# A second-stage projection as seven products of quarters in place of eight, and a new order at the seam of two stages

## The chip, the cores and the metric

The kernel runs on one core of one Trainium2 chip. The metric is the device time of one execution in microseconds (us). The kernel before takes 581.78 us, the median of three runs (581.43 to 581.80).

## What is computed

Three layers follow each other on 1536 tokens of 512 features, in float32. The first is a linear attention with decay. The second and third are what the change touches:

```
g = xn @ w_gate ; x = (g * sigmoid(g) * (xn @ w_val)) @ w_out           # 512 -> 1536 -> 512
h = max(x @ w1, x @ w2, x @ w3) ; out = h @ w_out2                      # 512 -> 768 -> 512
```

Every float32 operand is split in two float32r parts, a high one (a cast) and a low one (the rest), and each product of two operands is three matmuls: high with high, high with low, low with high.

## The kernel before, in words

The tokens lie in three blocks j of 512 columns. The first stage (gate, value and out) has 12 tiles f of 128 hidden features, the second (three projections and out) has 6. The list `steps` (L117 to L122) goes through groups of tiles and, in each group, through the blocks. One step of stage one is `hidden1` (L384), which makes two projections of 12 matmuls each, and `out1` (L409), 12 matmuls for the step ahead of it; one step of stage two is `hidden2` (L396), three projections of 12, and `out2` (L417), 12. Each matmul has a moving operand of 512 columns. `drain1` (L357) adds the four accumulator banks of a group to a running sum in SBUF; after the last group it also splits the block into its high part `yh` (ACT) and low part `yl` (POOL).

Work on the weights is woven in. `make_unit` (L142) moves each unit of weights, 128x512 words, through three calls: in the first ACT prepares the words (L173, L174), in the second DVE treats them three times (L153, L155, L157) and POOL adds (L159), in the third ACT casts the high part (L148) and POOL subtracts the low one (L149). It is called from `gap` (L323), which stands behind every second piece of six matmuls, at every fourth gap from step 4 on. `load_to` (L134) sends the weight loads through SP's queue, three units ahead.

Within each engine the order is the written one (`tc.manual_schedule()`, L460), and an instruction that waits holds up all that stand behind it on its engine. There are 8 PSUM banks in one pool (L60), each handed out again once its last reader is done. The split of a hidden tile (`split`, L349) is an ACT cast and a POOL subtraction, and `out1` of that tile needs both: its second matmul already reads the low part. `feed_forward` (L427) writes the order: hidden tile of this step, its split, and then the out-matmuls of the step before.

```
def mm3(out, wh, wl, xh_, xl_, first, last):
    nc.tensor.matmul(out=out, lhsT=wh, rhs=xh_, start=first, stop=False)
    nc.tensor.matmul(out=out, lhsT=wh, rhs=xl_, start=False, stop=False)
    nc.tensor.matmul(out=out, lhsT=wl, rhs=xh_, start=False, stop=last)
```

Of the kernel before, what the change touches and what calls it, by code (L numbers as in the profile page):

```python
# [12 lines left out]
ALU = mybir.AluOpType  # L13
# [13 lines left out]
def tile_decay_attention_swiglu_maxout(  # L27
# [23 lines left out]
    NB = 512  # L51
    WBUFS = 12
# [12 lines left out]
    wpools = [wp]  # L65

# [42 lines left out]
    unit_list = [(nm, f) for f in range(F1) for nm in "gvo"] + [(nm, f) for f in range(F2) for nm in "123p"]  # L109
    groups1, groups2 = [4, 2, 2, 2, 2], [2, 2, 2]  # L110
    group_of = {}
    for n0, groups, names in ((0, groups1, "gvo"), (len(groups1), groups2, "123p")):
        f0 = 0
        for g_, n_ in enumerate(groups):
            group_of.update({(nm, f): n0 + g_ for nm in names for f in range(f0, f0 + n_)})
            f0 += n_
    steps = []  # L117
    for stage_, groups in ((1, groups1), (2, groups2)):
        f0 = 0
        for g_, n_ in enumerate(groups):  # L120
            steps += [(stage_, g_, j_, f_, f0, f0 + n_ - 1) for j_ in range(NBLK) for f_ in range(f0, f0 + n_)]
            f0 += n_  # L122
    first_use = {}
    for i_, (stage_, _, _, f_, _, _) in enumerate(steps):
        for nm in ("gvo" if stage_ == 1 else "123p"):
            first_use.setdefault((nm, f_), i_)
# [3 lines left out]
    held = {}  # L130
    room = [WBUFS, 8]
    pos = {"load": 0, "made": 0, "step": 0, "gap": 0}

    def load_to(n):  # L134
        while pos["load"] < min(n, len(unit_list)):
            nm, f = unit_list[pos["load"]]
            t = wp.tile([P, KD, 2 * P], I32, tag="raw", name="wraw", bufs=3)
            nc.sync.dma_start(out=t, in_=source[nm](f))
            raws[nm, f] = t
            pos["load"] += 1  # L140

    def make_unit():  # L142

        if len(stage2):
            key, W, at = stage2.pop(0)
            wh = wpools[at].tile([P, 512], F32R, tag="wh", name="wh")
            wl = wpools[at].tile([P, 512], F32R, tag="wl", name="wl")
            nc.scalar.copy(out=wh, in_=W.bitcast(F32))  # L148
            nc.gpsimd.tensor_tensor(out=wl, in0=W.bitcast(F32), in1=wh.bitcast(F32), op=ALU.subtract)  # L149
            units[key] = (wh, wl)  # L150
        if len(stage1):
            key, W, at, lo, hi = stage1.pop(0)
            nc.vector.tensor_scalar(out=W.bitcast(F32), in0=W.bitcast(F32), scalar1=LEAST, scalar2=MOST,  # L153
                                    op0=ALU.max, op1=ALU.min)
            nc.vector.tensor_scalar(out=W, in0=W, scalar1=0x07FFFFFF, scalar2=3,  # L155
                                    op0=ALU.bitwise_and, op1=ALU.logical_shift_left)
            nc.vector.scalar_tensor_tensor(out=W, in0=hi, scalar=-0x40000000, in1=W,  # L157
                                           op0=ALU.bitwise_and, op1=ALU.bitwise_or)
            nc.gpsimd.tensor_tensor(out=W, in0=W, in1=lo, op=ALU.add)  # L159
# [5 lines left out]
        if first_use[key] <= pos["step"] + 6 and at < len(wpools) and room[at]:  # L165
            load_to(pos["made"] + (3 if pos["step"] else 1))
            room[at] -= 1
            held[key] = at
            pos["made"] += 1
            t = raws.pop(key).rearrange("p k (f w) -> p (k f) w", w=2)  # L170
            lo, hi = t[:, :, 0], t[:, :, 1]
            W = wp.tile([P, 512], I32, tag="W", name="W", bufs=3)
# [150 lines left out]
    def gap():  # L323


        pos["gap"] += 1
        if (pos["gap"] + 5) % (2 if pos["step"] < groups1[0] else 4) == 0:
# [27 lines left out]
    yb = {}  # L355

    def drain1(acc, g, j):  # L357
        if g == 0:
            acc_sb[j] = act.tile([P, KD, NB], F32, tag="acc", name="acc_sb", bufs=3)
            for m in range(KD):  # L360
                nc.scalar.copy(out=acc_sb[j][:, m, :], in_=acc[m])
            return
        for m in range(KD):
            nc.vector.tensor_tensor(out=acc_sb[j][:, m, :], in0=acc[m], in1=acc_sb[j][:, m, :], op=ALU.add)
        if g == len(groups1) - 1:
            yh = act.tile([P, KD, NB], F32R, tag="xh", name="yh", bufs=3)
            yl = act.tile([P, KD, NB], F32R, tag="xl", name="yl", bufs=3)
            for m in range(KD):
                split(yh[:, m, :], yl[:, m, :], acc_sb[j][:, m, :])
            yb[j] = (yh, yl)  # L370

    def drain2(acc, g, j):
        if g == 0:
            acc_sb[j] = act.tile([P, KD, NB], F32, tag="acc", name="acc_sb", bufs=3)
        for t in range(KD):
            if g == 0:
                nc.scalar.copy(out=acc_sb[j][:, t, :], in_=acc[t])
                continue
            nc.vector.tensor_tensor(out=acc_sb[j][:, t, :], in0=acc[t], in1=acc_sb[j][:, t, :], op=ALU.add)
            if g == len(groups2) - 1:  # L380
                r0 = j * NB + t * P
                nc.sync.dma_start(out=out[r0:r0 + P, :], in_=acc_sb[j][:, t, :])

    def hidden1(f, j):  # L384
# [4 lines left out]
        proj(pv, units["v", f], bh, bl)  # L389
# [5 lines left out]

    def hidden2(f, j):  # L396
        bh, bl = yb[j]
        ps = []
        for i in range(3):
            pw = bank(f"pw{i}")  # L400
            proj(pw, units["123"[i], f], bh, bl)
            ps.append(pw)
        m1 = act.tile([P, NB], F32, tag="sg", name="m1", bufs=1)
        nc.scalar.copy(out=m1, in_=ps[0])
        nc.vector.tensor_tensor(out=m1, in0=ps[1], in1=m1, op=ALU.max)  # L405
        nc.vector.tensor_tensor(out=m1, in0=ps[2], in1=m1, op=ALU.max)
        return m1
# [9 lines left out]
    def out2(acc, f, f0, f1, hh, hl):  # L417
        wh, wl = units["p", f]
        for t in range(NB // P):
            ts = slice(t * P, (t + 1) * P)  # L420
            nc.tensor.matmul(out=acc[t], lhsT=hh[:, ts], rhs=wh, start=f == f0, stop=False)  # L421
            nc.tensor.matmul(out=acc[t], lhsT=hh[:, ts], rhs=wl, start=False, stop=False)  # L422
            nc.tensor.matmul(out=acc[t], lhsT=hl[:, ts], rhs=wh, start=False, stop=f == f1)  # L423
            if t % 2:
                gap()

    def feed_forward():  # L427
        acc = []
        before = None
        for now in steps + [None]:  # L430
            if now:
                pos["step"] = steps.index(now)
                stage, g, j, f, f0, f1 = now
                if stage == 1 and g == 0 and f == f0:
# [7 lines left out]
                r = (hidden1 if stage == 1 else hidden2)(f, j)  # L442
# [3 lines left out]
            if before:  # L446
                stage, g, j, f, f0, f1, ph, pl = before
                if f == f0:
                    acc = [bank("acc") for _ in range(4)]
                (out1 if stage == 1 else out2)(acc, f, f0, f1, ph, pl)  # L450
                if f == f1:
                    (drain1 if stage == 1 else drain2)(acc, g, j)
                if j == NBLK - 1:
                    for nm in ("gvo" if stage == 1 else "123p"):
                        del units[nm, f]
                        room[held.pop((nm, f))] += 1
            if now:
                before = (*now, hh, hl)

    with tc.manual_schedule():  # L460
# [30 lines left out]
        feed_forward()  # L491
# [31 lines left out]
```

## Time and profile before

| | |
|---|---|
| median of three runs | 581.78 us |
| the profiled execution | 582.03 us |
| its span, first to last instruction | 580.2 us |
| PE busy / DVE / POOL / ACT | 563.9 / 341.4 / 292.7 / 223.4 us |
| 512-column matmuls, stage one / stage two | 1296 / 864 |
| TensorE's granted clock, mean | 0.996 of full speed |

A profile row of a group gives the line, the engine, the operation, the tile written and the tiles read, the count, the busy time with the mean of one in ns, and the idle time of the engine ahead of it with its releaser. A row of the timeline gives start, duration, engine, line and operation. A row of a window gives its bounds and length, then the busy time of PE, PE's weight loads, DVE, ACT and POOL, the granted clock, and the DMA share and rate. The modelled ends of matmuls overlap, so it is the distance of their starts that tells their pace.

### The profile page before, as it was taken

How to read it: one execution, taken by the hardware profiler on the slowest of the kernel's cores; microseconds unless marked ns; L12 is line 12 of the kernel's file. 1: busy time of each engine (PE TensorE's matmuls, PEld its weight loads, DVE VectorE, ACT ScalarE, POOL GpSimd, SP SyncE). 2: the span in 40 equal slices, each digit the busy share in tenths (PEclk: the TensorE clock that was granted, in tenths of full speed). 3: DMA queues.
4: the chain of work that ended last, by engine and by line, in shares of the span. 5: the costliest groups of instructions: out<-in, count | busy, mean ns of one | idle time of the engine just before them, and what ended most of it. 6: DMA issues, size and time to landing. Idle time of an engine off the chain costs nothing.

```text
span 580.2 us, 7727 instructions
## 1 busy us (share of the span) xinstructions
PE 563.9 (97%) x2970; PEld 466.5 (80%) x2970; DVE 341.4 (59%) x467; ACT 223.4 (38%) x422; POOL 292.7 (50%) x231
## 2 busy tenths in 40 slices
PE   7979898999999999999999999999999999999997
PEld 7868676888788888888888888888888888888885
DVE  6687996433556783775477388868732674321322
ACT  3656653432453642342253245553532533101100
POOL 2577988211356773365256257988741566110110
PEclk9998999999999999999999999999999999999999
DMA  9677554000033231132033022322321220000111
GB/s 213 169 194 193 143 163 128 1 2 0 2 108 110 73 108 37 36 104 78 0 111 105 4 72 73 109 74 73 108 73 37 69 77 2 0 0 1 74 72 73
DMA packets 64645, 44.54 MB, mean 77 GB/s; under 512 B 39264, under 2 KB 60768, under 8 KB 64608
## 3 DMA queue, kind: packets, MB, share of 16 engines
q1 hardware_dynamic: 63936, 44.05, 25.8%
q8 instruction: 23, 0.38, 0.3%
q14 instruction: 14, 0.11, 0.1%
q10 hardware_dynamic: 672, 0.01, 0.1%
HBM read 40.90 MB, written 3.15 MB: 76 GB/s over the span
## 4 chain that ended last, share of the span: by engine, by line
PE 87%; DVE 7%; DMA 2%; ACT 2%; issue 1%; SPq 0%; POOL 0%; DVEq 0%; ACTq 0%
PE pw L339 8%; PE pw L337 8%; PE pw L338 8%; PE acc L337 5%; PE pv L337 5%; PE pg L337 5%; PE pg L338 5%; PE pv L339 5%; PE acc L339 5%; PE pg L339 5%; PE acc L338 5%; PE pv L338 5%; PE acc L423 3%; PE acc L421 3%; PE acc L422 3%; PE px L244 2%
## 5 line engine op out<-in xcount | busy, mean ns | idle before, releaser
L149 POOL TENSOR_TENSOR wl<-W,wh 128x512 fp32r<-128x512 f32 x60 | 90.7, 1511 | 21.1 <-ACT wh L148 21.1
L351 POOL TENSOR_TENSOR hl<-sg,hh 128x512 fp32r<-128x512 f32 x36 | 47.3, 1314 | 101.3 <-ACT hh L350 98.4
L159 POOL TENSOR_TENSOR W<-W,wraw 128x512 int32<-128x512 int32 x60 | 80.1, 1335 | 17.9 <-DVE W L157 13.0
L157 DVE SCALAR_TENSOR_TENSOR W<-wraw,W 128x512 int32<-128x512 int32 x60 | 84.3, 1405 | 2.1
L337 PE MATMUL pw<-yh,wh 128*128 128x512 f32 x216 | 84.0, 389 | 0.0
L338 PE MATMUL pw<-yl,wh 128*128 128x512 f32 x216 | 84.0, 389 | 0.0
L339 PE MATMUL pw<-yh,wl 128*128 128x512 f32 x216 | 84.0, 389 | 0.0
L351 POOL TENSOR_TENSOR hl<-m,hh 128x512 fp32r<-128x512 f32 x18 | 23.3, 1294 | 102.3 <-ACT hh L350 102.3
L392 DVE TENSOR_TENSOR sg<-pg,sg 128x512 f32<-128x512 f32 x36 | 24.7, 687 | 60.2 <-ACT sg L391 60.2
L337 PE MATMUL pv<-xh,wh 128*128 128x512 f32 x144 | 57.1, 397 | 1.0 <-DVE x L300 1.0
L337 PE MATMUL pg<-xh,wh 128*128 128x512 f32 x144 | 58.0, 403 | 0.1
L148 ACT CAST wh<-W 128x512 fp32r<-128x512 f32 x60 | 37.2, 619 | 54.4 <-POOL W L159 54.3
L338 PE MATMUL pg<-xl,wh 128*128 128x512 f32 x144 | 56.7, 394 | 0.5 <-DVE xl L311 0.5
L339 PE MATMUL pg<-xh,wl 128*128 128x512 f32 x144 | 56.7, 394 | 0.3 <-POOL wl L149 0.3
L337 PE MATMUL acc<-hh,wh 128*128 128x512 f32 x144 | 56.9, 395 | 0.0
L350 ACT CAST hh<-sg 128x512 fp32r<-128x512 f32 x36 | 22.4, 622 | 88.9 <-DVE sg L393 88.9
L339 PE MATMUL pv<-xh,wl 128*128 128x512 f32 x144 | 56.2, 390 | 0.0
L339 PE MATMUL acc<-hh,wl 128*128 128x512 f32 x144 | 56.1, 390 | 0.0
L338 PE MATMUL acc<-hl,wh 128*128 128x512 f32 x144 | 56.1, 390 | 0.0
L338 PE MATMUL pv<-xl,wh 128*128 128x512 f32 x144 | 56.1, 390 | 0.0
L405 DVE TENSOR_TENSOR m<-pw,m 128x512 f32<-128x512 f32 x18 | 12.4, 691 | 70.6 <-PE pw L339 59.8
L153 DVE TENSOR_SCALAR W<-W 128x512 f32<-128x512 f32 x60 | 42.6, 710 | 9.2 <-POOL hl L351 4.8
(84 smaller groups left out, 1063.3 us busy)
## 6 DMA issues: line engine op xcount, KB each, us to landing
wraw<-in_moe_w_out_dram SPq DMA_DIRECT2D x18, 512.0 KB, 3.3
wraw<-in_moe_w_dram SPq DMA_DIRECT2D x18, 512.0 KB, 3.5
wraw<-in_moe_w_gate_dram SPq DMA_DIRECT2D x12, 512.0 KB, 3.6
wraw<-in_moe_w_val_dram SPq DMA_DIRECT2D x12, 512.0 KB, 3.6
kn<-in_k_dram SPq DMA_DIRECT2D x12, 256.0 KB, 4.0
qn<-in_q_dram SPq DMA_DIRECT2D x12, 256.0 KB, 4.4
vn<-in_v_dram SPq DMA_DIRECT2D x12, 256.0 KB, 4.7
out_dram<-acc_sb SPq DMA_DIRECT2D x12, 256.0 KB, 2.1
```

What stands on the lines that cost most here:

```text
L148: nc.scalar.copy(out=wh, in_=W.bitcast(F32))
L149: nc.gpsimd.tensor_tensor(out=wl, in0=W.bitcast(F32), in1=wh.bitcast(F32), op=ALU.subtract)
L153: nc.vector.tensor_scalar(out=W.bitcast(F32), in0=W.bitcast(F32), scalar1=LEAST, scalar2=MOST, op0=ALU.max, op1=ALU.min)
L157: nc.vector.scalar_tensor_tensor(out=W, in0=hi, scalar=-0x40000000, in1=W, op0=ALU.bitwise_and, op1=ALU.bitwise_or)
L159: nc.gpsimd.tensor_tensor(out=W, in0=W, in1=lo, op=ALU.add)
L337: nc.tensor.matmul(out=out, lhsT=wh, rhs=xh_, start=first, stop=False)
L338: nc.tensor.matmul(out=out, lhsT=wh, rhs=xl_, start=False, stop=False)
L339: nc.tensor.matmul(out=out, lhsT=wl, rhs=xh_, start=False, stop=last)
L350: nc.scalar.copy(out=dst_h, in_=src)
L351: nc.gpsimd.tensor_tensor(out=dst_l, in0=src, in1=dst_h.bitcast(F32), op=ALU.subtract)
L392: nc.vector.tensor_tensor(out=sg, in0=pg, in1=sg, op=ALU.mult)
L421: nc.tensor.matmul(out=acc[t], lhsT=hh[:, ts], rhs=wh, start=f == f0, stop=False)
```

## The change

Stage two takes two tiles of hidden features together (a pair g, three pairs), and for each of the three projections i (a round, nine of them) it takes blocks 0 and 1 as one matrix of two by two quarters: two halves of the 512 features by two blocks. Seven products of quarters with sums (a Strassen scheme in Winograd's form) replace eight; block 2 is still done directly, as four products. A product is six matmuls.

The sums on the side of the weights are units "T1", "T2", "T3": four subtractions of 128x256 on DVE for a pair, written over the words of the two raw units, then cast and split as another unit. The sums on the side of the tokens are made once, at the seam (`sums_of_quarters`): for each half k of a quarter, four sums on DVE, five high parts on ACT, three low parts on POOL and two on DVE. The banks of the last accumulation of block 1 hold two of the four sums. The recombination of the seven products is partly in PSUM, with an intermediate copied out by ACT (`held_back`), and partly an addition on DVE; the maximum over the three projections then has both inputs in SBUF in three of the six tiles of a pair.

At the seam `out1` of (block 1, tile 11) runs in the middle of the value projection of (block 2, tile 10); the sums for k=0 follow at once, those for k=1 only behind the hidden tile of (block 2, tile 11). The flag `quiet` stops `make_unit` from there until `out1` of (block 2, tile 11) is issued.

```diff
+    unit_list += [("1", 0), ("1", 1), None, ("T1", 0), ("T1", 1), ("2", 0), ("2", 1), None, ("T2", 0), ("T2", 1),
+                  ("3", 0), ("3", 1)]
+    for f in range(0, F2 - 2, 2):
+        unit_list += [("1", f + 2), ("T3", f), ("T3", f + 1), ("1", f + 3), ("p", f), ("T1", f + 2), ("T1", f + 3),
+                      ("p", f + 1), ("2", f + 2), ("2", f + 3), ("3", f + 2), ("T2", f + 2), ("T2", f + 3), ("3", f + 3)]
+    unit_list += [("p", F2 - 2), ("T3", F2 - 2), ("T3", F2 - 1), ("p", F2 - 1)]
...
+            elif key and key[1] % 2 == 0:
+                a, b = W.bitcast(F32), words[key[0][1], key[1] + 1].bitcast(F32)
+                for o, x, y in ((a[:, :HF], b[:, :HF], a[:, :HF]), (b[:, :HF], b[:, HF:], b[:, :HF]),
+                                (b[:, HF:], b[:, HF:], a[:, :HF]), (a[:, HF:], a[:, HF:], b[:, HF:])):
+                    nc.vector.tensor_tensor(out=o, in0=x, in1=y, op=ALU.subtract)
...
-    def gap():
+    later = []
+
+    def gap(make=None):
...
+        if make and not pos["quiet"]:
             make_unit()
+        if later and not pos["quiet"]:
+            later.pop(0)()
...
-    def proj(ps, unit, bh, bl):
+    def proj(ps, unit, bh, bl, between=None):
         wh, wl = unit
         for kk in range(KD):
+            if between and kk == KD // 2:
+                between()
...
+        def sums(k):
+            s3, s4 = (wpools[1].tile([P, NB], F32, tag=("wh", "wl")[k], name="sums") for _ in range(2))
+            for nm, t, a, b, op in (("s3", s3, y0[:, k, :], ps[k], ALU.subtract), ("s1", ps[k], ps[k], y[:, 2 + k, :], ALU.add),
+                                    ("s2", ps[2 + k], ps[k], y0[:, k, :], ALU.subtract),
+                                    ("s4", s4, y0[:, 2 + k, :], ps[2 + k], ALU.subtract)):
+                nc.vector.tensor_tensor(out=t, in0=a, in1=b, op=op)
+                src[nm, k] = t
+            src["22", k] = y[:, 2 + k, :]
+
+        def high(k):
+            for nm in ("s1", "s2", "s4", "s3", "22"):
+                h_, _, o = Y[nm]
+                nc.scalar.copy(out=h_[:, o + k, :], in_=src[nm, k])
+            for nm in ("s4", "s3", "22"):
+                low(nm, k, nc.gpsimd)
...
+        sums(0)
+        high(0)
+        low("s1", 0, nc.vector)
+        later.append(lambda: low("s2", 0, nc.vector))
+        later.append(lambda: (sums(1), high(1), low("s1", 1, nc.vector), low("s2", 1, nc.vector)))
+        pos["quiet"] = True
...
+                early = before and g == len(groups1) - 1 and before[1:3] == (1, f1)
+                r = hidden1(f, j, finish if early else None)
                 hh = act.tile([P, NB], F32R, tag="hh", name="hh")
                 hl = act.tile([P, NB], F32R, tag="hl", name="hl")
                 split(hh, hl, r)
...
+                if later:
+                    later.pop(0)()
+                if before and not early:
+                    finish()
...
+    def add_max(ps, c, i, key, n):
+
+        if i == 0:
+            nc.vector.tensor_tensor(out=hidden_tile(key, n), in0=ps, in1=c, op=ALU.add)
+            return
+        nc.vector.tensor_tensor(out=c, in0=ps, in1=c, op=ALU.add)
+        nc.vector.tensor_tensor(out=hid[key], in0=hid[key], in1=c, op=ALU.max)
+        if i == 2:
+            halves(key)
...
+        elif n == 7:
+            product(ps_of[at, "p"], t1, 0, Y["s3"], False)
+            add_max(ps_of[at, "p"], ps_of.pop((at, "m5")), i, (1, 1), 1)
+        elif n == 2:
+            q_ = bank("q")
+            product(q_, u0, 1, Y["12"], True)
+            add_max(q_, ps_of.pop((at, "c1")), i, (0, 0), 2)
+        elif n == 4:
+            p = ps_of.pop((at, "p"))
+            product(p, t0, 1, Y["22"], False)
+            just_max(p, i, (1, 0), 3)
...
+        gap(n in (5, 2, 7) or g == 0 and n == (1, 1))
...
+        first, second = (0, 0), (0, 1)
+        work = [(first, 1), (first, 2), first_end, (first, 5), (first, 6), (second, 1), (first, 3), (first, 7),
+                (second, 2), (first, (0, 0)), (first, 4), (second, 5), (first, (0, 1)), (second, 6), (first, (1, 0)),
+                (second, 3), (first, (1, 1)), (second, 7), (second, (0, 0)), (second, (0, 1)), (second, 4),
+                (second, (1, 0)), (second, (1, 1))]
+        for g in range(F2 // 2):
+            for i in range(3):
+                if g or i == 2:
+                    work += [((g, i), n) for n in (1, 5, (0, 0), (0, 1), 6, 2, 3, 7, (1, 0), (1, 1), 4)]
+                if g and i == 0:
+                    work.append(lambda g=g: out2(g - 1))
+        work.append(lambda: out2(F2 // 2 - 1))
```

`first_end` is `out1` and the drain of (block 2, tile 11). `out2` now takes both tiles of a pair into one bank, six matmuls, and adds it to the running sum bank by bank. `held_back` is one ACT copy out of PSUM; products 1, 5 and 6 have it.

## Rows read from the trace of the kernel before

**Rows 1.** The page's first part: busy time, share of the span, instructions of each engine.

```profile
PE 563.9 (97%) x2970; PEld 466.5 (80%) x2970; DVE 341.4 (59%) x467; ACT 223.4 (38%) x422; POOL 292.7 (50%) x231
```

**Rows 2.** Windows: stage one without attention, and stage two's beginning.

```profile
160.00:375.00 215.00, 215.00 (x950) 177.94 (x950) 142.04 (x186) 87.73 (x155) 125.69 (x91) 1.00 0.23 74
375.00:440.00 65.00, 65.00 (x288) 53.85 (x287) 39.26 (x43) 27.98 (x51) 44.58 (x33) 1.00 0.26 82
```

**Rows 3.** Timeline of PE: the first matmuls of two neighbouring steps, 36 matmuls apart.

```profile
345.00 0.39 PE L337 MATMUL pg<-xh,wh 128*128 128x512 f32 x1
...
353.16 0.39 PE L337 MATMUL pg<-xh,wh 128*128 128x512 f32 x1
```

**Rows 4.** Groups by line: one of the three matmul groups of each projection kind.

```profile
L337 PE MATMUL pw<-yh,wh 128*128 128x512 f32 x216 | 84.0, 389 | 0.0
...
L421 PE MATMUL acc<-wh,hh 128*128 128x512 f32 x72 | 28.0, 389 | 0.0
```

**Rows 5.** Timeline: the end of the kernel.

```profile
574.43 2.74 DVE L379 TENSOR_TENSOR acc_sb<-acc,acc_sb 128x512 f32<-128x512 f32 x4 [2.72 <-PE acc L423]
...
576.06 0.39 PE L423 MATMUL acc<-wh,hl 128*128 128x512 f32 x1
```

**Rows 6.** Groups by line: what a hidden tile's chain and a drain are made of.

```profile
L391 ACT ACTIVATE sg<-pg 128x512 f32<-128x512 f32 x36 | 21.3, 591 | 43.3 <-PE pg L339 43.3
...
L393 DVE TENSOR_TENSOR sg<-pv,sg 128x512 f32<-128x512 f32 x36 | 24.9, 692 | 23.7 <-PE pv L339 22.1
...
L350 ACT CAST hh<-sg 128x512 fp32r<-128x512 f32 x36 | 22.4, 622 | 88.9 <-DVE sg L393 88.9
...
L351 POOL TENSOR_TENSOR hl<-sg,hh 128x512 fp32r<-128x512 f32 x36 | 47.3, 1314 | 101.3 <-ACT hh L350 98.4 <-issue 2.9
...
L364 DVE TENSOR_TENSOR acc_sb<-acc,acc_sb 128x512 f32<-128x512 f32 x48 | 30.4, 681 | 0.0
...
L351 POOL TENSOR_TENSOR yl<-acc_sb,yh 128x512 fp32r<-128x512 f32 x12 | 17.6, 1497 | 0.0
```

**Rows 7.** DVE's three word treatments: min/median/max in ns, then their groups' means.

```profile
L153 DVE TENSOR_SCALAR W<-W x60: 411/419/1516, 24.9 to 484.6; 128x512 f32<-128x512 f32 x60
...
L155 DVE TENSOR_SCALAR W<-W x60: 426/428/1421, 25.3 to 485.0; 128x512 int32<-128x512 int32 x60
...
L157 DVE SCALAR_TENSOR_TENSOR W<-wraw,W x60: 691/1726/1811, 26.5 to 485.5; 128x512 int32<-128x512 int32 x60
...
L157 DVE SCALAR_TENSOR_TENSOR W<-wraw,W 128x512 int32<-128x512 int32 x60 | 84.3, 1405 | 2.1
L153 DVE TENSOR_SCALAR W<-W 128x512 f32<-128x512 f32 x60 | 42.6, 710 | 9.2 <-POOL hl L351 4.8 <-ACT W L173 4.4
L155 DVE TENSOR_SCALAR W<-W 128x512 int32<-128x512 int32 x60 | 42.8, 713 | 2.1
```

**Rows 8.** DVE with two inputs: in SBUF both, one in PSUM, and half as wide.

```profile
L311 DVE TENSOR_TENSOR xl<-x,xh x4: 681/693/967, 112.9 to 148.2; 128x512 fp32r<-128x512 f32 x4
...
L405 DVE TENSOR_TENSOR m<-pw,m x18: 683/692/693, 386.4 to 568.4; 128x512 f32<-128x512 f32 x18
...
L269 DVE TENSOR_TENSOR S_kv<-pS,Sd 64x256 f32<-64x256 f32 x16 | 6.7, 421 | 8.7 <-PE pS L262 8.6
```

**Rows 9.** Groups by line: POOL's share of a unit of weights.

```profile
L149 POOL TENSOR_TENSOR wl<-W,wh 128x512 fp32r<-128x512 f32 x60 | 90.7, 1511 | 21.1 <-ACT wh L148 21.1
...
L159 POOL TENSOR_TENSOR W<-W,wraw 128x512 int32<-128x512 int32 x60 | 80.1, 1335 | 17.9 <-DVE W L157 13.0 <-ACT m L404 1.6 <-ACT wraw L174 1.6
```

**Rows 10.** Windows with a thin PE, and the granted clock behind the first.

```profile
39.00:43.00 4.00, 2.46 (x26) 2.03 (x26) 3.74 (x8) 1.39 (x3) 2.22 (x3) 1.00 1.15 290
43.00:47.00 4.00, 4.00 (x17) 3.41 (x15) 3.14 (x3) 2.29 (x5) 3.17 (x3) 0.57 0.83 189
70.00:72.00 2.00, 0.27 (x5) 0.28 (x7) 2.00 (x3) 1.22 (x3) 2.00 (x2) 1.00 0.16 50
93.00:96.00 3.00, 1.55 (x13) 0.95 (x13) 2.40 (x4) 0.48 (x1) 2.30 (x2) 1.00 1.21 263
```

More of the change, by code (lines that the diff above doesn't have):

```diff
@@ L51, in tile_decay_attention_swiglu_maxout @@
     NB = 512
+    HF = 2 * P
     WBUFS = 12
@@ L108, in tile_decay_attention_swiglu_maxout @@
               "1": cols(w1), "2": cols(w2), "3": cols(w3), "p": rows(w_out2)}
[L109 to L116, printed above, removed]
-    steps = []
[L118 to L126, printed above, removed]
+    unit_list = [(nm, f) for f in range(F1) for nm in "gvo"]
+    unit_list += [("1", 0), ("1", 1), None, ("T1", 0), ("T1", 1), ("2", 0), ("2", 1), None, ("T2", 0), ("T2", 1),
[4 more added lines that the diff above has]
+    unit_list += [("p", F2 - 2), ("T3", F2 - 2), ("T3", F2 - 1), ("p", F2 - 1)]
+    raw_list = [key for key in unit_list if key and key[0][0] != "T"]
+    groups1 = [4, 2, 2, 2, 2]
+    group_of = {key: int(key in (("T2", 0), ("T2", 1), ("3", 0), ("3", 1))) for key in unit_list}
+    steps = []
+    f0 = 0
+    for g_, n_ in enumerate(groups1):
+        group_of.update({(nm, f): g_ for nm in "gvo" for f in range(f0, f0 + n_)})
+        steps += [(g_, j_, f_, f0, f0 + n_ - 1) for j_ in range(NBLK) for f_ in range(f0, f0 + n_)]
+        f0 += n_
+    first_use = {key: len(steps) - 6 for key in unit_list}
+    for i_, (_, _, f_, _, _) in reversed(list(enumerate(steps))):
+        first_use.update({(nm, f_): i_ for nm in "gvo"})
     raws = {}
@@ L130, in tile_decay_attention_swiglu_maxout @@
     held = {}
+    words = {}
     room = [WBUFS, 8]
[L132 removed]
+    pos = {"load": 0, "made": 0, "raw": 0, "step": 0, "gap": 0, "quiet": False}
     def load_to(n):
[L135 to L136 removed]
+        while pos["load"] < min(n, len(raw_list)):
+            nm, f = raw_list[pos["load"]]
             t = wp.tile([P, KD, 2 * P], I32, tag="raw", name="wraw", bufs=3)
@@ L354, in tile_decay_attention_swiglu_maxout, with lower @@
     acc_sb = {}
-    yb = {}
+    Y = {}
+    def lower(eng, dst_h, dst_l, src):
+        eng.tensor_tensor(out=dst_l, in0=src, in1=dst_h.bitcast(F32), op=ALU.subtract)
     def drain1(acc, g, j):
@@ L362, in drain1 @@
             return
-        for m in range(KD):
[L364 to L382, printed above, removed]
@@ L384, in hidden1 @@
-    def hidden1(f, j):
+        y = acc_sb[j]
+        keep = g == len(groups1) - 1 and j == 1
+        for m in (0, 2, 1, 3) if keep else range(KD):
+            nc.vector.tensor_tensor(out=acc[m] if keep and m < 2 else y[:, m, :], in0=acc[m], in1=y[:, m, :], op=ALU.add)
+        if g < len(groups1) - 1:
+            return
+        if keep:
+            sums_of_quarters(list(acc), y)
+            return
+        yh = act.tile([P, KD, NB], F32R, tag="xh", name="yh", bufs=3)
+        yl = act.tile([P, KD, NB], F32R, tag="xl", name="yl", bufs=3)
@@ L385, in hidden1 @@
+    def hidden1(f, j, between=None):
         bh, bl = x_block(j)
@@ L388, in hidden1 @@
         pv = bank("pv")
-        proj(pv, units["v", f], bh, bl)
+        proj(pv, units["v", f], bh, bl, between)
+        if j == NBLK - 1:
+            free(("g", f), ("v", f))
         sg = act.tile([P, NB], F32, tag="sg", name="sg", bufs=1)
@@ L394, in hidden1 @@
         return sg
[L396 to L407, printed above, removed]
     def out1(acc, f, f0, f1, hh, hl):
@@ L415, in out1, with first_stage @@
                 gap()
[L417 to L427, printed above, removed]
+    def first_stage():
         acc = []
         before = None
-        for now in steps + [None]:
+        for now in steps:
             if now:
                 pos["step"] = steps.index(now)
-                stage, g, j, f, f0, f1 = now
-                if stage == 1 and g == 0 and f == f0:
+                g, j, f, f0, f1 = now
+                if g == 0 and f == f0:
                     while attn_q and attn_q[0][0] <= 6 + 4 * j:
@@ L445, in feed_forward @@
                 split(hh, hl, r)
[L446 to L456, printed above, removed]
@@ L457, in feed_forward, with finish @@
-            if now:
-                before = (*now, hh, hl)
+                if later:
+                    later.pop(0)()
+                if before and not early:
+                    finish()
+                def finish(now=now, hh=hh, hl=hl):
+                    g, j, f, f0, f1 = now
+                    if f == f0:
+                        acc[:] = [bank("acc") for _ in range(4)]
+                    out1(acc, f, f0, f1, hh, hl)
+                    if f == f1:
+                        drain1(acc, g, j)
+                    if j == NBLK - 1:
+                        free(("o", f))
@@ new lines, in first_stage, with free, product @@
+            before = now
+        return finish
+    def free(*keys):
+        for key in keys:
+            del units[key]
+            room[held.pop(key)] += 1
+    hid = {}
+    parts = {}
+    def product(ps, unit, half, x, first):
+        wh, wl = unit
+        xh_, xl_, o = x
+        for k in range(2):
+            ks = slice((2 * half + k) * P, (2 * half + k + 1) * P)
+            for n, (w, r) in enumerate(((wh, xh_), (wh, xl_), (wl, xh_))):
+                nc.tensor.matmul(out=ps, lhsT=w[:, ks], rhs=r[:, o + k, :], start=first and k == 0 and n == 0,
+                                 stop=k == 1 and n == 2, skip_group_check=True)
@@ new lines, in hidden_tile, with halves, do @@
+    def hidden_tile(key, n):
+        pool, tag, bufs = (act, "hh", 2) if n < 2 else (act, "hl", 2) if n < 4 else (act, "sg", 1) if n < 5 else (
+            wpools[1], "wl", 8)
+        hid[key] = pool.tile([P, NB], F32, tag=tag, name="m", bufs=bufs)
+        return hid[key]
+    def halves(key):
+        def do(m):
+            hh = wpools[1].tile([P, NB], F32R, tag="wh", name="hh2")
+            hl = wpools[1].tile([P, NB], F32R, tag="wl", name="hl2")
+            split(hh, hl, m)
+            parts[key] = (hh, hl)
+        later.append(lambda m=hid.pop(key): do(m))
@@ new lines, in pair_units, with held_back, piece @@
+    def pair_units(g, i):
+        nm = "123"[i]
+        for _ in range(9):
+            if ("T" + nm, 2 * g + 1) not in units:
+                make_unit()
+        return [units[k, 2 * g + d] for k in (nm, "T" + nm) for d in range(2)]
+    def held_back(ps, tag):
+        c = wpools[1].tile([P, NB], F32, tag=tag, name="c")
+        nc.scalar.copy(out=c, in_=ps)
+        return c
+    ps_of = {}
+    done = {}
+    def piece(g, i, n):
+        u0, u1, t0, t1 = pair_units(g, i)
+        at = g, i
+        if n == 1:
+            ps_of[at, "p"] = p = bank("p")
+            product(p, u0, 0, Y["11"], True)
+            ps_of[at, "c1"] = held_back(p, "wh")
+        elif n == 5:
+            ps_of[at, "r"] = r = bank("r")
+            product(r, t0, 0, Y["s1"], True)
+            ps_of[at, "m5"] = held_back(r, "wh")
+        elif n == 6:
+            product(ps_of[at, "p"], t1, 1, Y["s2"], False)
+            ps_of[at, "u2"] = held_back(ps_of[at, "p"], "wl")
+        elif n == 3:
+            r = ps_of.pop((at, "r"))
+            product(r, u1, 1, Y["s4"], False)
+            add_max(r, ps_of.pop((at, "u2")), i, (0, 1), 0)
+        elif n == 7:
[9 more added lines that the diff above has]
+            just_max(p, i, (1, 0), 3)
+        else:
+            d, half = n
+            yh, yl = Y["2"]
+            if half == 0:
+                ps_of[at, n[0]] = bank("p2")
+            product(ps_of[at, d], (u0, u1)[d], half, (yh, yl, 2 * half), half == 0)
+            if half:
+                just_max(ps_of.pop((at, d)), i, (2, d), 4 + d)
+        done[at] = done.get(at, 0) + 1
+        if done[at] == 11:
+            free(*((k + "123"[i], 2 * g + e) for k in ("", "T") for e in range(2)))
+        gap(n in (5, 2, 7) or g == 0 and n == (1, 1))
@@ new lines, in out2 @@
+    def out2(g):
+        last = g == F2 // 2 - 1
+        for j in range(NBLK):
+            if g == 0:
+                acc_sb[j] = act.tile([P, KD, NB], F32, tag="acc", name="acc_sb", bufs=3)
+            for t in range(NB // P):
+                ts = slice(t * P, (t + 1) * P)
+                acc = bank("acc")
+                for d in range(2):
+                    wh, wl = units["p", 2 * g + d]
+                    hh, hl = parts[j, d]
+                    nc.tensor.matmul(out=acc, lhsT=hh[:, ts], rhs=wh, start=d == 0, stop=False)
+                    nc.tensor.matmul(out=acc, lhsT=hh[:, ts], rhs=wl, start=False, stop=False)
+                    nc.tensor.matmul(out=acc, lhsT=hl[:, ts], rhs=wh, start=False, stop=d == 1)
+                y = acc_sb[j][:, t, :]
+                if g == 0:
+                    nc.scalar.copy(out=y, in_=acc)
+                else:
+                    nc.vector.tensor_tensor(out=y, in0=acc, in1=y, op=ALU.add)
+                if last:
+                    r0 = j * NB + t * P
+                    nc.sync.dma_start(out=out[r0:r0 + P, :], in_=y)
+                gap(t % 2 == 1)
+        free(("p", 2 * g), ("p", 2 * g + 1))
@@ new lines, in second_stage, with first_end @@
+    def second_stage(finish):
+        def first_end():
+            finish()
+            pos["quiet"] = False
+        first, second = (0, 0), (0, 1)
[10 more added lines that the diff above has]
+        work.append(lambda: out2(F2 // 2 - 1))
+        for w in work:
+            if callable(w):
+                w()
+            else:
+                piece(*w[0], w[1])
@@ L490, in tile_decay_attention_swiglu_maxout @@
                 make_unit()
-        feed_forward()
+        finish = first_stage()
+        pos["step"] = len(steps)
+        second_stage(finish)
 _INS = ['q', 'k', 'v', 'lam', 'moe_w_gate', 'moe_w_val', 'moe_w_out', 'moe_rms_g',
```

67 lines of the change are left out of this document (54 added, 13 removed).

## The prediction

> **What bounds the kernel now.** First the page's busy times: PE 563.9 us of a span of 580.2, DVE 341.4, POOL 292.7, ACT 223.4 [rows 1]. A busy PE could still hide waits, so next the windows: from 160 us on PE is busy without a break, in stage one (215.0 of 215.0) as at the start of stage two (65.0 of 65.0), and the granted clock is 1.00, that is 2.4 GHz [rows 2]. Then the pace: two neighbouring steps start their first matmul at 345.00 and 353.16, 36 matmuls apart, so a 512-column matmul costs 8.16 / 36 = 0.2267 us [rows 3]; the 389 ns of a group's mean is the modelled length, and the starts are what count [rows 4]. So from 160 us on the time is the number of matmuls times 0.2267, plus a tail: the last matmul starts at 576.06, the last addition ends at 574.43 + 2.74 = 577.17 and the last store is out at 580.2 [rows 5]. Any work that PE doesn't wait for is free, and any wait of PE is paid in full.
>
> **What is removed.** Stage two has 648 projection matmuls (three groups of 216) and 216 out-matmuls (three of 72) [rows 4]. A round (one projection, two tiles) now takes 7 + 4 = 11 products of six instead of 12: 66 for 72. Nine rounds save 54 matmuls: 54 x 0.2267 = 12.24 us. Stage one, the out-matmuls and the tail stay: the last bank is still followed by one addition of 0.68 us and one store. The weight loads are the same 24, in another order, on SP's queue with nothing behind them; the twelve stores leave in the same last step.
>
> **The seam.** Counting matmuls from the trace of before, the gate projection of (block 2, tile 10) starts at 353.16 + 8.16 = 361.32. Now 18 matmuls later, at 365.40, comes `out1` of (block 1, tile 11) until 368.12, then the rest of the value projection until 369.48, then 24 matmuls of tile 11 until 374.92. There `out1` of (block 2, tile 10) is wanted; its first matmul needs the high part of that hidden tile, its second, at 375.15, the low part. What stands ahead of these two parts on their engines:
> - DVE: four drains of 0.68 behind the banks, the last ending at about 369.5, then four sums in a chain; s1 is ready at 371.0 and s4 at 372.4 (0.69 each, as an addition with one input in PSUM [rows 8]).
> - ACT: five high parts of 0.62, of which the third waits for s4: 372.4 + 3 x 0.6 = 374.2. Only behind them the sigmoid, 374.8; then two DVE products of 0.69, 376.3; then the cast, 377.0 [rows 6].
> - POOL: three low parts from 373.1 on, 1.3 each, until 377.0; then the low part of the hidden tile, 378.4 [rows 6].
>
> So PE starts one matmul at 377.0 and the next at 378.4 in place of 375.15: **3.3 us lost**. The ends: with all POOL work at the drain's 1.50 [rows 6] it is 4.1; if the sums' chain runs at the drains' spacing and PE's second wait overlaps it, 2.5. Behind that the seam is covered: 23 matmuls (5.2 us) follow before `out1` of tile 11 needs its parts, which POOL has at 378.4 + 1.3 + 1.3 = 381; the sums for k=1 are done on DVE at about 383.3, and product 5, the first to read them, stands at 386.6. No weights are begun for 66 matmuls, 15 us plus the stall; the first pair's twelve units are ready before that, and by the written order no round must make a unit at its own start.
>
> **The rounds.** All that is added here lies beside PE as long as it is in time. ACT gets 27 copies out of PSUM and 18 casts, 27 x 0.59 + 18 x 0.62 = 27 us over 180; POOL 18 subtractions of 1.51 [rows 9], 27 us. The narrow engine is DVE. From the seam to the last unit of weights PE has 630 matmuls, 142.8 us, and DVE must do there: 18 raw units, 28 half-width subtractions for the T units, 13 maxima with both inputs in SBUF, and 50 additions, maxima and drains with an input in PSUM, 50 x 0.69 = 34.5 us. Rows of before have no half-width subtraction and only four two-input operations in SBUF of this kind, so they get bounds. A raw unit costs 0.41 + 0.43 + 0.69 = 1.5 us at the least, 2.8 in the mean, 4.7 at the worst [rows 7]; such a maximum 0.69 (median of L311) up to the 1.81 of L157, which has two SBUF inputs too [rows 7, 8]; a subtraction 0.42 (the 256-wide row [rows 8]) up to 0.42 + 1.12, the surcharge of L157's worst. The sum is 82 us at the floor, 126 in the middle (2.8, 1.4 and 0.82), 185 at the ceiling, for 142.8. In the middle DVE is 88% full, so what matters is where PE waits for it.
>
> That place is one. Product 4 accumulates into the bank that product 7 has filled, and must wait until DVE has added product 7's result out of it. From the end of product 2 to that start there are 24 matmuls, 5.44 us. In them DVE must do three additions, two SBUF maxima and, in some rounds, the word treatment that the call of `make_unit` behind product 2 issues: 2.07 + 2 x 1.05 + 2.5 (the three medians, L153 to L157, less their overlap) = 6.7, or 1.2 us late; by the means 2.07 + 2.8 + 2.8 = 7.7, 2.2 late; at the floor 5.0, not late. Going through the unit list with the gaps, two rounds have a raw unit there (third round of the first pair, second of the second), the others none, or T subtractions in a first round, which has no maxima. A backlog is carried into two more (first round of the second pair, behind two raw units; second of the third, behind an `out2` with twelve additions and four units), worth 0 to 1.3 each. Medians give 2 x 1.35 = 2.7 us, means 5.3. I take **4.0 us**, in the middle, because L157's mean was measured with POOL 126 / 215 = 58% busy in stage one [rows 2] and POOL will be at about 68% here (98 us of 142.8: 18 units of 2.85, 14 T, 12 splits, drains and low parts). The floor is 0; the ceiling is the whole overfull DVE, 185 - 143 = 42.
>
> [...]
>
> **The sum**, against the profiled execution of 582.03 us: 582.03 - 12.24 + 3.3 + 4.0 = 577.1. That execution lies 0.25 above the median of the runs, so I say **576.8**.
>
> **The rivals.**
> - *All behind the seam is covered.* DVE is on time, only the seam is lost: 582.03 - 12.24 + 3.3 - 0.25 = 572.8. For it: no wait of PE in before's stage one, where DVE was 142 / 215 = 66% busy [rows 2]; against it: 88% here. Chance 0.20.
> - *DVE becomes the bound, and the kernel is slower.* The place is the bank between products 7 and 4; it decides once more than 12.24 - 3.3 = 8.9 us are lost there. With maxima and subtractions always at the ceiling and raw units at the mean: 34.5 + 23.5 + 42 + 51 = 151, 8 us more than PE's 142.8, plus some 4 us in which DVE itself waits for products to end: 12 lost, 584.8. For it: more than half of L157's 60 lie near its ceiling (its median of 1726 ns does [rows 7]); against it: the maxima come one by one, not in a row behind operations that let POOL in between. Chance 0.19. [...]
> - *No difference.* The waits come to between 8 and 10 us: the forecast's, with the clock lost at the seam on top. In the thin stretch from 39 to 43 us (PE busy 2.46 of 4.0) the clock fell behind it to 1.2 GHz for most of 4 us (0.57), which costs about 2 us; after 0.27 of 2.0 us and 1.55 of 3.0 it held [rows 10]. The seam leaves PE with about 0.2 of 3.5 us. 581 to 583. Chance 0.11.
>
> The forecast, waits behind the seam of 2 to 8 us and 574.8 to 580.8, has the remaining 0.50.
>
> **The numbers.** About 0.2%, 1.2 us, is what a measurement of this kernel tells from no change. Faster by more than that are the forecast and the covered case, 0.70; the same 0.11; slower 0.19. The range goes from 571.5 (nothing late, a seam of 2.0) to 585.0 (the slower rival's own price); the cases with a fuller DVE lie beyond it.
>
> **What would show it.** 2106 matmuls of 512 columns in place of 2160, at 0.2267. At about 375 us one stall of PE in two parts, the first ending on ACT's cast of the hidden tile, the second on POOL's low part, 3.3 us together; a granted clock of 1.00 behind it. In the rounds, PE waiting for a DVE addition at the start of product 4, in the third round of the first pair and the second of the second above all, 1 to 2 us each. The SBUF maxima near 1.1 and the subtractions near 0.8 us. The prediction is wrong if PE waits elsewhere (weights not ready, ACT's copies out of PSUM late behind a cast that waits for POOL), if the seam's stall is under 2 or over 5 us, or if the waits for DVE come to nothing or to over 8.

## The result, and the profile after

The changed kernel takes 584.99 us (median of four runs, 583.61 to 585.56) where the kernel before, run beside it, takes 581.79: a ratio of 1.0052, 95% interval 1.0032 to 1.0073. It is slower by half a per cent; 576.8 was forecast. The profiled execution is the fastest of the four, 583.61 us, against 582.03 before: 1.58 more. Its mean granted clock is 0.991, the others' 0.988. The other three have no trace, so the 1.4 us from this execution to the median aren't split up below.

First the page of the changed kernel, then its waits of PE from 160 us on (engine, line and releaser; us in total, times, longest).

```profile
span 581.8 us, 7768 instructions
PE 557.2 (96%) x2916; PEld 457.9 (79%) x2916; DVE 392.9 (68%) x542; ACT 247.0 (42%) x464; POOL 320.0 (55%) x251
...
PEclk9999999999999999999999999989997999999999
```

```profile
PE p L534 <- ACT c L578: 4.1, 1, 4.1
PE acc L367 <- ACT hh L382: 2.1, 1, 2.1
PE acc L368 <- POOL hl L383: 0.8, 1, 0.8
PE p L534 <- DVE c L556: 0.8, 2, 0.5
```

PE has 54 instructions fewer [rows 1], so the products are saved. Before, PE had no wait here [rows 2]; now it has three kinds (for ACT's copy ahead of a product, for the hidden tile's parts at the seam, for a DVE addition), and the clock drops in two slices. From the distances of PE's starts beyond 0.2267 us, the profiled execution reads:

| | us |
|---|---|
| 54 matmuls | -12.24 |
| seam: the hidden tile's high part 2.23, low part 1.11 | +3.3 |
| ahead of product 6, first round of the second pair | +4.2 |
| ahead of product 4, three times: 0.69, 0.42, 0.28 | +1.4 |
| matmuls slowed behind the seam and behind product 6's wait (9 and 14, most at 1.2 GHz and 0.427), and small rests | +4.5 |
| restarts (the second matmul behind a wait is late by 0.1 to 0.36) | +0.8 |
| arrival at the seam | -0.8 |

That is +1.2; PE's last matmul starts 1.34 later than before [rows 5]. The last row is luck and no gain of the change: the code of the attention stage is the same, but behind the thin stretch of the attention stage the granted clock was 0.57 in the trace of before [rows 10] and 1.00 here:

```profile
43.00:47.00 4.00, 4.00 (x34) 3.36 (x33) 3.42 (x3) 2.27 (x5) 3.28 (x3) 1.00 0.72 163
```

From the last projection matmul of stage one (374.75 before, 373.91 here) to the end of the span it is 205.5 us before and 207.9 now: 2.4 more.

The seam, by the timelines of DVE, ACT and POOL in the changed kernel:

```profile
370.71 0.69 DVE L435 TENSOR_TENSOR sums<-acc_sb,acc 128x512 f32<-128x512 f32 x1
...
371.92 1.14 ACT L442 CAST xh<-sums 128x512 fp32r<-128x512 f32 x2
372.96 0.62 ACT L442 CAST ah<-acc_sb 128x512 fp32r<-128x512 f32 x1
373.48 0.60 ACT L466 ACTIVATE sg<-pg 128x512 f32<-128x512 f32 x1
375.70 0.62 ACT L382 CAST hh<-sg 128x512 fp32r<-128x512 f32 x1 [1.62 <-DVE sg L468]
...
375.10 1.27 POOL L390 TENSOR_TENSOR al<-acc_sb,ah 128x512 fp32r<-128x512 f32 x1
376.39 1.26 POOL L383 TENSOR_TENSOR hl<-sg,hh 128x512 fp32r<-128x512 f32 x1
```

It is the chain that was forecast: sums, five casts, only then the sigmoid, the tile's high part at 376.3 and, behind three low parts, its low part at 377.65. The second stall, by the timelines of DVE and ACT, ends with `c`, the copy of product 1, out of whose bank product 6 (start 440.08) accumulates:

```profile
429.84 1.52 DVE L163 TENSOR_SCALAR W<-W 128x512 f32<-128x512 f32 x1
431.39 1.40 DVE L165 TENSOR_SCALAR W<-W 128x512 int32<-128x512 int32 x1
432.82 0.69 DVE L167 SCALAR_TENSOR_TENSOR W<-wraw,W 128x512 int32<-128x512 int32 x1
433.43 0.68 DVE L565 TENSOR_TENSOR m<-p,m 128x512 f32<-128x512 f32 x1
434.03 1.15 DVE L163 TENSOR_SCALAR W<-W 128x512 f32<-128x512 f32 x1
435.22 1.40 DVE L165 TENSOR_SCALAR W<-W 128x512 int32<-128x512 int32 x1
436.65 1.64 DVE L167 SCALAR_TENSOR_TENSOR W<-wraw,W 128x512 int32<-128x512 int32 x1
438.21 0.68 DVE L565 TENSOR_TENSOR m<-p,m 128x512 f32<-128x512 f32 x1
...
434.93 0.62 ACT L157 CAST wh<-W 128x512 fp32r<-128x512 f32 x1 [3.88 <-POOL W L169]
...
438.92 0.62 ACT L382 CAST hh<-m 128x512 fp32r<-128x512 f32 x1 [1.73 <-DVE m L565]
439.45 0.58 ACT L578 COPY c<-p 128x512 f32<-128x512 f32 x1
```

Read it from below. The copy stands in ACT's order behind the cast of product 4's tile, which waits for DVE's maximum, which stands behind two word treatments of 3.6 and 4.2 us, in place of a mean of 2.8 [rows 7]. Product 1 itself had long been done: its last matmul starts at 431.53. The windows show the bunch:

```profile
386.00:424.00 38.00, 38.00 (x169) 31.45 (x168) 23.91 (x35) 18.85 (x33) 21.22 (x17) 1.00 0.13 42
424.00:443.00 19.00, 14.39 (x57) 11.16 (x56) 18.65 (x19) 8.27 (x15) 15.13 (x12) 0.91 0.27 83
```

DVE is 63% busy for 38 us, then 98% for 19, with POOL at 80%.

### The profile page after: what moved, and what is told of

Its sections match the earlier page's. It is cut to its first block, busy times and chain, and to the rows that moved or that the text cites. A ratio compares the mean times of both kernels' runs of the same rounds, so it can differ in the third digit from the quotient of the medians.

```text
span 581.8 us, 7768 instructions
## 1 busy us (share of the span) xinstructions
PE 557.2 (96%) x2916; PEld 457.9 (79%) x2916; DVE 392.9 (68%) x542; ACT 247.0 (42%) x464; POOL 320.0 (55%) x251
## 4 chain that ended last, share of the span: by engine, by line
PE 79%; DVE 12%; issue 2%; ACT 2%; DMA 2%; POOL 2%; SPq 0%; DVEq 0%; POOLq 0%; ACTq 0%
PE p L534 14%; PE acc L367 5%; PE acc L368 5%; PE acc L369 5%; PE pg L367 5%; PE pv L367 5%; PE pg L368 5%; PE pv L369 5%; PE pg L369 5%; PE pv L368 5%; PE r L534 4%; PE acc L639 3%; PE acc L640 3%; PE acc L638 3%; PE q L534 2%
## 5 line engine op out<-in xcount | busy, mean ns | idle before, releaser
L158 POOL TENSOR_TENSOR wl<-W,wh 128x512 fp32r<-128x512 f32 x78 | 113.5, 1455 | 54.2 <-ACT wh L157 54.2
L157 ACT CAST wh<-W 128x512 fp32r<-128x512 f32 x78 | 48.3, 620 | 86.0 <-POOL W L169 73.5
L163 DVE TENSOR_SCALAR W<-W 128x512 f32<-128x512 f32 x60 | 43.2, 721 | 6.5 <-ACT W L197 6.4
L165 DVE TENSOR_SCALAR W<-W 128x512 int32<-128x512 int32 x60 | 41.5, 692 | 2.1
L197 ACT ACTIVATE W<-wraw 128x512 f32<-128x512 f32 x60 | 40.2, 670 | 2.6 <-POOL wl L158 2.6
L468 DVE TENSOR_TENSOR sg<-pv,sg 128x512 f32<-128x512 f32 x36 | 24.9, 692 | 22.4 <-PE pv L369 20.7
L198 ACT ACTIVATE wraw<-wraw 128x512 int32<-128x512 uint32 x60 | 39.8, 664 | 0.0
L383 POOL TENSOR_TENSOR hl<-m,hh 128x512 fp32r<-128x512 f32 x18 | 27.1, 1522 | 18.5 <-ACT hh L382 18.4
```

## The experiments

Each edit is made to the changed kernel. The theories: "queue" (the order on ACT is at fault), "full" (DVE has more to do in that round than the round is long), "blocked" (its treatments are long because POOL and DVE block each other), and "idle" for the clock. All ratios are to the kernel before, run beside each (its median there was 581.8 to 582.9 us); gains in us are differences to the changed kernel's 585.0, beside which the kernel before took 581.79.

**The split one gap later.**

```diff
-        gap(n in (5, 2, 7) or g == 0 and n == (1, 1))
+        gap(n in (5, 2, 7) or g == 0 and n == (1, 1), n != 4)   # False: no late split in this gap
```

> Edit: the split of product 4's hidden tile is issued one gap later, so that ACT copies product 1 of the next round out of PSUM ahead of that cast. Theory 'queue' (DVE's backlog reaches PE because the copy stands behind a cast that waits for DVE): the wait of 4.2 us ahead of product 6 in the first round of the second pair falls to about 1.6 (what is left stands behind the cast of a weight that waits for POOL), the clock doesn't fall behind it (2.8 us); the time falls from 585.0 by 3 to 5.5 us. Theory 'full' (DVE has too much to do there whatever the order): the wait turns up at another place, at most 1 us is won.

Measured: 584.78 us, ratio 1.0058 (1.0039 to 1.0077), nothing won. Its waits of PE:

```profile
PE p L534 <- DVE m L554: 3.1, 1, 3.1
PE acc L367 <- ACT hh L382: 2.1, 1, 2.1
PE p L534 <- ACT c L578: 1.7, 1, 1.7
...
```

The wait for ACT's copy falls to 1.7, as "queue" has it, but 3.1 us appear at product 4 of the same round, where DVE's addition comes late. ACT's order chooses the place; DVE's lateness is what is paid.

**A call moved out of the third round.**

```diff
-        gap(n in (5, 2, 7) or g == 0 and n == (1, 1))
+        gap(n in (5, 2, 7) or (g, i) in ((0, 0), (0, 1), (1, 0)) and n == (1, 1))
```

> Edit: one of the four calls that move the weights on in the third round of the first pair is made in the next round instead, so that one treatment of words (4.3 us there, blocked by POOL) leaves DVE's backlog. Theory 'full' (DVE has more to do in that round than the round is long): the wait of 4.2 us ahead of product 6 falls under 0.5 us, no wait takes its place, and the clock's 2.8 us behind it come back: 6 to 7 us less than the changed kernel's 585.0, so 578 to 579. Rival (DVE is late by the mean of the whole stage, not by this round): the wait moves to the first round of the second pair, at most 2 us less.

Measured: 579.68 us, ratio 0.9951 (0.9933 to 0.9969). Its waits of PE from 160 us on, all of them:

```profile
PE acc L367 <- ACT hh L382: 2.1, 1, 2.1
PE acc L368 <- POOL hl L383: 0.9, 1, 0.9
PE p L534 <- DVE c L556: 0.8, 2, 0.5
```

The wait for the copy is gone, and by the starts no other took its place with more than 0.25 us. One call less in one round wins 5.3 us (6 to 7 were expected): "full" holds, as a matter of that round. A call brings work for ACT and POOL too, so this run doesn't tell DVE's own work from POOL's blocking; the run without POOL's low parts, below, does.

**The parts of the sums behind the hidden tile.**

```diff
         sums(0)
-        high(0)
-        low("s1", 0, nc.vector)
-        later.append(lambda: low("s2", 0, nc.vector))
+        later.append(lambda: (high(0), low("s1", 0, nc.vector), low("s2", 0, nc.vector)))
```

> Edit: at the seam only the four sums for k=0 stay ahead of the hidden tile of (block 2, tile 10); their five high parts on ACT and the low parts go behind that tile's split. Theory 'queue': the waits of 2.2 and 1.1 us for the tile's high and low part fall to 0.6 us together and the clock doesn't fall behind them (1.5 us): 4 to 4.8 us less, about 580.6. Rival: the parts are then late for product 5, which waits in their place; at most 1.5 us less.

Measured: 581.18 us, ratio 0.9980 (0.9965 to 0.9996), 3.8 less than the changed kernel. The seam's waits are one of 0.4 for the low part, and a new one of 0.5 at product 5; its clock doesn't fall.

**A fill in the seam's wait.** In `finish`, behind the allocation of the banks of (block 2, tile 10):

```diff
+                            for _ in range(14):
+                                nc.tensor.matmul(out=acc[0], lhsT=units["o", f][0][:, 0:P], rhs=x_block(j)[0][:, 0, :],
+                                                 start=True, stop=True)
```

> Edit: 14 matmuls with no use go to PE in the wait at the seam (3.2 us at 0.2267), into a bank that the next real matmul overwrites. If PE's idling is what lets the clock fall behind the seam, the granted clock stays 1.00 there, the wait for the low part ends where it did, and 1.5 us are won: 583.5. If the clock falls for another reason, nothing is won, and the fill may cost up to 1 us: 585 to 586.

Measured: 581.54 us, ratio 0.9989 (0.9974 to 1.0005), 3.4 less. Windows at the seam, first with the fill, then the changed kernel:

```profile
373.00:378.00 5.00, 4.96 (x23) 3.79 (x22) 1.98 (x3) 1.98 (x5) 4.82 (x4) 1.00 0.00 0
378.00:382.00 4.00, 4.00 (x18) 3.27 (x19) 3.34 (x6) 1.13 (x3) 1.29 (x1) 1.00 0.02 4
```

```profile
373.00:378.00 5.00, 2.08 (x8) 1.23 (x7) 1.98 (x3) 2.00 (x5) 4.63 (x4) 1.00 0.00 0
378.00:382.00 4.00, 4.00 (x12) 3.09 (x12) 3.51 (x6) 1.13 (x3) 1.28 (x1) 0.58 0.02 4
```

The clock holds at 1.00 where it fell to 0.58, so here idling is what lets it fall; with the seam's waits down to 0.4 us, in the run above, it doesn't fall there either. The gain is above the 1.5 expected: the clock behind the second wait also fell for only 6 matmuls in place of 14, which nothing in the edit explains.

**Weights begun at the seam.**

```diff
-        if make and not pos["quiet"]:
+        if make:
```

> Edit: weights are begun at the seam as elsewhere (the flag holds back only the late sums, no longer the units); all units come three to four calls earlier. Theory 'displaced work' (the units not begun at the seam pile up on DVE in the third round of the first pair): the wait of 4.2 us there and its 2.8 us of clock go, the seam's waits grow by at most 1.5 us: 580 to 582. Rival (holding back the weights pays): the seam's waits grow by more than is won behind; 585 or more.

Measured: 585.84 us, ratio 1.0071 (1.0055 to 1.0086). The seam is unchanged (2.1 and 0.8), and the wait for the copy grows to 5.2. The theory of displaced work falls, and the rival, whose range holds the time, isn't the reason either, as the seam's waits didn't grow: earlier units bring the four subtractions of the next T unit into the third round, where they take 5.38 us together.

**All sums at once.** `sums`, `high` and both DVE low parts for k = 0 and 1 in one block ahead of the last tile.

> Edit: both halves of the sums at the seam go ahead of the last tile of stage one, as one block (undoes the change's 'ahead of half of the sums'). Theory: ACT's five and POOL's three parts for k=1 then also stand ahead of the sigmoid and the low part of the hidden tile: 3 x 1.3 us on POOL more, the two waits at the seam grow from 3.3 to about 7 us, with a longer fall of the clock: 588 to 590. Rival (the late half is as dear behind the last tile as ahead of it): 585 to 586.

Measured: 587.99 us, ratio 1.0105 (1.0082 to 1.0128). The wait for the high part grows from 2.1 to 6.1, the rest stays. So putting half of the sums behind the last tile is worth 3 us; it puts too little there.

**Together.** First parts and call:

> Edits: the parts of the sums for k=0 behind the hidden tile's split, and the call moved out of the third round; together. If the two losses are independent, both gains add: 585.0 - 3.8 - 6.5 = 574.7, that is 7 us or 1.2% below the kernel before. If DVE only hands its lateness on, at least one of the gains is lost: 578 to 581.

Measured: 575.84 us, ratio 0.9892 (0.9874 to 0.9909). The gains add: 585.0 - 3.8 - 5.3 = 575.9. The split one gap later on top:

> Edits: as the two together, and the split of product 4's tile one gap later as well. With DVE no longer late in the third round that order is worth nothing more: within 0.7 us of the two together. If ACT's queue is a limit of its own, 1 us or more below it.

Measured: 576.82 us, 0.9899 (0.9882 to 0.9917). It is 1.0 above the two, a little more than the 0.7 allowed, but from the seam on the traces differ by only 0.1 us (table below). Nothing is won: ACT's order matters only while DVE is late.

**POOL's low parts left out.** In `halves`, for the first pair, `parts[key] = (hh, hh)` without POOL's subtraction.

> Edit: the changed kernel, with the six low parts that POOL makes of the first pair's hidden tiles left out (the high part is read in their place, so those products lack their low part). It takes 6 x 1.3 us or more from POOL in the third round and nothing from DVE. Theory 'blocked' (DVE's treatments are long there because POOL and DVE block each other): the two treatments of 3.6 and 4.3 us shrink to 2.6 or less each and the wait of 4.2 us ahead of product 6 to 1.5 us or less; 578.5 to 581. Rival (the number of DVE's instructions is what counts): the wait stays over 3 us, 584 to 585.5.

Measured: 579.84 us, ratio 0.9963 (0.9942 to 0.9984). Its wait for the copy, and DVE over the same stretch:

```profile
PE p L534 <- ACT c L586: 1.8, 1, 1.8
```

```profile
429.42 0.42 DVE L163 TENSOR_SCALAR W<-W 128x512 f32<-128x512 f32 x1
429.87 1.40 DVE L165 TENSOR_SCALAR W<-W 128x512 int32<-128x512 int32 x1
431.31 0.69 DVE L167 SCALAR_TENSOR_TENSOR W<-wraw,W 128x512 int32<-128x512 int32 x1
...
432.52 1.15 DVE L163 TENSOR_SCALAR W<-W 128x512 f32<-128x512 f32 x1
433.71 0.43 DVE L165 TENSOR_SCALAR W<-W 128x512 int32<-128x512 int32 x1
434.17 1.79 DVE L167 SCALAR_TENSOR_TENSOR W<-wraw,W 128x512 int32<-128x512 int32 x1
```

The same instructions take 2.5 and 3.4 us in place of 3.6 and 4.2, and the wait for the copy falls from 4.1 to 1.8. No DVE instruction was removed, so a good half of that wait is POOL blocking DVE. The second treatment missed the 2.6 expected of each, and the wait is a little above the 1.5.

**Maxima with an input in PSUM.**

```diff
-        nc.vector.tensor_tensor(out=c, in0=ps, in1=c, op=ALU.add)
-        nc.vector.tensor_tensor(out=hid[key], in0=hid[key], in1=c, op=ALU.max)
+        t = c if n == 1 else ps
+        nc.vector.tensor_tensor(out=t, in0=ps, in1=c, op=ALU.add)
+        nc.vector.tensor_tensor(out=hid[key], in0=t, in1=hid[key], op=ALU.max)
```

> Edit: the changed kernel, with the sums of products 2 and 3 written back to their PSUM bank, so that 12 of the 18 maxima have one input in SBUF and one in PSUM. Theory 'blocked': these twelve take 0.69 us in place of 0.96 in the mean; the waits for DVE ahead of product 4 (0.7, 0.4, 0.3) go, the wait ahead of product 6 loses 0.5 to 1.5 us: 582.5 to 584.5. Rival (the maxima's price plays no part): 585 within 0.7.

Measured: 581.45 us, ratio 0.9987 (0.9967 to 1.0006). First the maxima of the changed kernel, then two of the groups here:

```profile
L557 DVE TENSOR_TENSOR m<-m,c x18: 692/1026/1379, 397.3 to 558.2; 128x512 f32<-128x512 f32 x18
```

```profile
L558 DVE TENSOR_TENSOR m<-q,m x6: 690/691/695, 399.3 to 554.4; 128x512 f32<-128x512 f32 x6
L558 DVE TENSOR_TENSOR m<-r,m x6: 691/691/696, 408.0 to 555.8; 128x512 f32<-128x512 f32 x6
```

The price is as expected and every wait ahead of product 4 is gone; the wait for the copy stays at 4.2, against the expectation, since PE now comes to it 1.0 us earlier, by what it no longer loses, and the copy's end only 0.9 earlier. The time lies below the 582.5 to 584.5 expected, and about half of the 3.5 us isn't shown to be the edit's: in the profiled execution 12 matmuls ran at the lower clock in place of 20, and the edit explains the waits of 1.4 alone, with their restarts of 0.3.

**All three that help.**

> Edits: the parts of the sums behind the split, the call moved, and the maxima of products 2 and 3 with an input in PSUM. Theory 'blocked': against the first two together (575.8) the waits ahead of product 4 go, 1 to 1.5 us: 574.5. Rival: 575.8 within 0.7.

Measured: 573.94 us, ratio 0.9851 (0.9820 to 0.9882). Its waits of PE from 160 us on:

```profile
PE r L532 <- ACT c L577: 0.4, 1, 0.4
PE acc L368 <- POOL hl L383: 0.4, 1, 0.4
```

This beats both kernels: 8.9 us under the one before, run beside it (582.85), with 0.8 us of such waits left of 7.8. The executions also differ ahead of the seam, where their code is the same. This table leaves that out: it runs from the last projection matmul of stage one to the end of the profiled execution's span.

| kernel | us |
|---|---|
| before | 205.5 |
| changed | 207.9 |
| split one gap later | 207.7 |
| call moved | 202.4 |
| first parts behind the tile | 204.5 |
| fill at the seam | 204.9 |
| weights begun at the seam | 210.0 |
| all sums at once | 211.5 |
| parts and call together | 198.8 |
| the two, and the split later | 198.9 |
| no low parts on POOL | 204.3 |
| maxima with an input in PSUM | 204.8 |
| all three that help | 197.2 |

The gains of the parts (3.4) and of the call (5.5) add here too, to 9.1; the maxima on top bring 1.6.

## Why the prediction was wrong

- *Saved matmuls, 12.24 us.* Right: 54 instructions fewer, and the same pace wherever the clock is full.
- *Seam, 3.3 us.* Right in place, chain and size: 2.23 + 1.11 = 3.34. Not right is the "granted clock of 1.00 behind it", see below.
- *"All that is added here lies beside PE ..., that place is one."* This step failed. Product 4's bank is a place, and cost 1.4 us: in the two rounds named and in one more, the first of the third pair. The large loss, 4.2 us, came at product 6 through ACT's order, at a copy whose own data was ready, behind a cast that waited for DVE. The prediction had a like path (a copy behind a cast that waits for POOL) only among the things that would prove it wrong, without a price.
- *Rounds, 4.0 us.* Mis-sized, because it was made by the mean. (Its ends, 2.7 and 5.3, don't follow from the 1.2 and 2.2 us late that stand ahead of them: twice that is 2.5 and 4.5, before any backlog.) The prices were if anything too high: the SBUF maximum measured 0.96 for 1.4, the half-width subtraction 0.71 for 0.82, a raw unit 2.8 as taken. But the rounds' own balance was the one to make: 4 calls fall in the third round of the first pair, which has splits on POOL as well, and there DVE is 98% full and a treatment costs 3.6 to 4.2. The waits came to 5.6, with restarts over 6.
- *The clock, nothing in the forecast, 2 us in a rival.* This step failed too: the sum has no term for it, though the prediction had read a fall to 0.57 behind a thin stretch [rows 10]. It took 4.5 us, in two places, and the fill shows for the seam that PE's idling is what brings it. This is the largest missing term: with 3.3, 5.6, 0.8 and 4.5 the savings are more than used up.
- *The slower rival* gave 584.8 and the median is 585.0, but by half a coincidence: its 12 us of waits for DVE at product 4 were 5.6, and the clock made up the rest. Its mechanism, POOL blocking DVE, is shown by the run without POOL's low parts. The Trainium skill, "SBUF — State Buffer", section "Who interferes with whom", states that a DVE instruction with two SBUF inputs contends with a GpSimd (POOL) instruction that reads SBUF, and that one with at most one SBUF input doesn't outside the 2-port modes, which a `tensor_scalar` can enter. The runs agree: the maxima took 1026 ns at the median with two SBUF inputs and 691 with one, and L163, a `tensor_scalar` with one, took 1.52 us in the full round and 0.42 at the same place without POOL's low parts. But the rival's ceiling prices were too high, 1.81 us a maximum for a mean of 0.96; what counted was where POOL was busy.

What stays open: how much of the idle DVE time from 386 to 424 us could take weights; only one order of starting them earlier was tried, and it made the third round fuller.

## What to carry to other kernels

An engine that is 88% full on average needs its balance made round by round, with the prices of that round: move one piece of work out of the fullest round before changing anything else. Ahead of a copy that frees a PSUM bank, look at what stands before it on its engine and what that waits for; and put into a chain towards PE (sigmoid, product, split) nothing that is needed only 15 us later. Where PE must wait for some us, the wait's price is the wait plus the clock behind it; matmuls of no use kept the clock at the one place where they were tried.

## What the hardware showed that was not expected

The clock fell to 1.2 GHz behind the seam's 2.1 and 0.8 us of waiting, where the kernel before had held it at 1.00 in and behind thin stretches of 2 and 3 us (from 70 and from 93 us [rows 10]). A single wait of 1.7 us was followed by a full clock in the kernel with the later split, one of 1.8 us in the kernel without low parts by a granted clock of 0.67 from 440 to 444 us. Behind nearly the same wait of 4.1 to 4.2 us, between 6 and 14 matmuls ran at the lower level. So the price of a stall varies from run to run by more than a microsecond, and part of the spread between runs of these kernels is that. Another part lies ahead of anything the change touches: in the twelve profiled executions of the changed kernel and its variants the last projection matmul of stage one starts between 373.8 and 376.6 us.
